# A small gMLP stage beside a stream of K and V loads: x made the stationary operand, one product per group for the row sums

## The chip, the cores and the metric

The kernel runs on one core of a Trainium2 chip. The metric is the device time of one execution in microseconds (us), taken as the median of several executions. All executions told of here were classed as undisturbed (fast); executions of one kernel lie within some 2 us of each other. A ratio below is of one kernel's fast runs to the other's in the same rounds, with a 95% interval; it isn't quite the ratio of the medians quoted beside it. The profile is of one execution; its span is about 2 us shorter than the device time. In its lines PE is TensorE (PEld its weight loads), DVE VectorE, ACT ScalarE, POOL GpSimd and SPq the queue of the sync engine; the clock is the share of TensorE's full clock that it was granted.

## The reference, cut to what matters

One decode step: a layer norm of x (4 rows of 640), then an attention over long caches and a gated MLP side by side, both added to x.

```python
# caches: k, v are (4, 32, 4096, 128) bf16: 268 MB together
q = (xn @ wq).reshape(4, 1, 32, 128).transpose(0, 2, 1, 3)
p = softmax(einsum('bhqd,bhkd->bhqk', q, k_cache) * 128 ** -0.5)
A = einsum('bhqk,bhkd->bhqd', p, v_cache)...reshape(4, 1, 4096) @ wo
z = gelu(xn @ w_in)                      # w_in: 640 x 1728
z1, z2 = z[..., :864], layernorm(z[..., 864:])
B = (z1 * (w_sp * z2 + b_sp)) @ w_out    # w_out: 864 x 640
out = x + A + B
```

The kernel calls the product that w_out multiplies u.

## The kernel before: the parts concerned

The queue of the sync engine loads all but x and two small vectors, in this order: wq, w_in, w_out, then K and V in units of 8 MB (128 rows of 64 KB), and wo. K, V and the weights share five slots of a buffer, so a load can be issued only when the last reader of its slot is done. The gMLP, with 120 small products:

```python
FA = 5                                   # w_out: 5 rows of 640 to each of 128 partitions,
FR = (Fh - FA * P) // 32                 # the rest (7 rows) to each of 32 partitions
...
nc.sync.dma_start(out=w_out, in_=B_w_out[0:nf, :].rearrange("(p c) n -> p c n", p=P))
w_rest_d = B_w_out[nf:Fh, :].rearrange("(i r c) n -> r i c n", r=4, c=FR)
for r in range(4):
    nc.sync.dma_start(out=w_rest[r:32:4], in_=w_rest_d[r])      # 8 rows each
...
zT_ps = misc_ps([P, 2, FC, B], F32)
for part in range(2):
    for fc in range(FC):
        ...
        for c in range(DC):              # w: a strided column block of w_in, stationary
            nc.tensor.matmul(zT_ps[:n, part, fc, :], lhsT=w, rhs=xnT[:, c, 0:B], ...)
nc.scalar.activation(out=zT[:, :, 0:FA, :], in_=zT_ps[:, :, 0:FA, :], func=ACT.Gelu_apprx_tanh)
...                                      # statistics with a ones matrix, Sqrt, u = z1 * t1
etab = const.tile([P, 1], F32)           # loads the Exp table early
nc.scalar.activation(out=etab[:], in_=rs[:, 0:1], func=ACT.Exp)
```

The softmax of a group and what follows it, on whose end the V loads hang:

```python
nc.scalar.activation(out=p_bf[:, :, e, :], in_=S_ps[:, e], func=ACT.Exp, ...)   # per e
nc.vector.transpose(pT[...], p_bf[...])
... # 16 copies pT -> xd, 16 masked copies xd -> Zb (z_fill): VectorE has 11 and 3, ScalarE 5 and 13
for e in range(NE):
    nc.tensor.matmul(cs[:], lhsT=SelPe[:, e]..., rhs=rowsum[:, e:e + 1], ...)
nc.vector.reciprocal(out=rinv[:], in_=cs[:])
```

Of the kernel before, what the change touches and what calls it, by code (L numbers as in the profile page):

```python
# [8 lines left out]
ACT = mybir.ActivationFunctionType  # L9
ALU = mybir.AluOpType  # L10
AX = mybir.AxisListType
F32 = mybir.dt.float32
BF16 = mybir.dt.bfloat16
# [3 lines left out]
def kernel(  # L17
# [19 lines left out]
    nc = tc.nc  # L37
    P = 128
# [5 lines left out]
    HP = 4  # L44
# [9 lines left out]
    G = HG * B  # L54
    F2 = B_w_in.shape[1]
    Fh = F2 // 2
    FA = 5
    FR = (Fh - FA * P) // 32
    assert Fh == FA * P + FR * 32
    FC = FA + FR  # L60
# [20 lines left out]
    def misc_ps(shape, dtype):  # L81
        misc_ctr[0] += 1
        return ps_m.tile(shape, dtype, tag="misc", name=f"misc{misc_ctr[0]}")
# [5 lines left out]
    def at_slot(i, n, off=0):  # L89
        return kv[:, i * SL + off:i * SL + off + n]  # L90
# [12 lines left out]
    nc.scalar.dma_start(out=sb_bf[:, 0:1], in_=B_w_sp)  # L103
    nc.scalar.dma_start(out=sb_bf[:, 1:2], in_=B_b_sp[None, :])

    x_res = const.tile([32, NO2], BF16)
    nc.gpsimd.memset(x_res[:], 0.0)

    wq = at_slot(0, n_q).rearrange("p (c n) -> p c n", c=DC)
# [7 lines left out]
    nc.sync.dma_start(out=w_out, in_=B_w_out[0:nf, :].rearrange("(p c) n -> p c n", p=P))  # L117
    w_rest_t = ktpool.tile([P, NKT], F32, tag="kT", name="w_rest")
    w_rest = w_rest_t[:32].bitcast(BF16)[:, 0:FR * NOUT].rearrange("p (c n) -> p c n", c=FR)
    w_rest_d = B_w_out[nf:Fh, :].rearrange("(i r c) n -> r i c n", r=4, c=FR)  # L120
    for r in range(4):
        nc.sync.dma_start(out=w_rest[r:32:4], in_=w_rest_d[r])
# [88 lines left out]
    for q in range(4):  # L211
        nc.vector.tensor_copy(out=I32[32 * q:32 * q + 32, :], in_=ident_f[32 * q:32 * q + 32, 32 * q:32 * q + 32])

    SelP = const.tile([P, HP * B], F32)
    nc.vector.tensor_reduce(out=SelP[:], in_=I32[:].rearrange("p (pr c) -> p pr c", c=C2), axis=AX.X, op=ALU.add)
    SelN = const.tile([P, HP * B], F32)
    nc.vector.tensor_scalar(out=SelN[:], in0=SelP[:], scalar1=-scale, scalar2=None, op0=ALU.mult)
    SelPe = const.tile([P, NE, HP, NE, B], F32)
    nc.gpsimd.memset(SelPe[:].rearrange("p x h e b -> p (x h e b)"), 0.0)
    for e in range(NE):  # L220
        nc.vector.tensor_copy(out=SelPe[:, e, :, e, :], in_=SelP[:].rearrange("p (h b) -> p h b", b=B))

    SelH = const.tile([P, HG], F32)
    nc.vector.tensor_reduce(out=SelH[:], in_=I32[:].rearrange("p (h c) -> p h c", c=4), axis=AX.X, op=ALU.add)
# [12 lines left out]

    MkH = const.tile([G, HG], F32)
    nc.vector.tensor_reduce(out=MkH[:], in_=ident_f[:G, :G].rearrange("p (h b) -> p h b", b=B), axis=AX.X, op=ALU.add)
    B32f = const.tile([G, B], F32)  # L240
    nc.vector.tensor_reduce(out=B32f[:], in_=ident_f[:G, :G].rearrange("p (h b) -> p b h", b=B), axis=AX.X, op=ALU.add)
    B32 = const.tile([G, B], BF16)
# [30 lines left out]
    nc.vector.tensor_copy(out=qT[:], in_=q4[:, 1, :].rearrange("p (h k r) -> p h k r", h=HG, k=4)[:, :, :, 0:B])  # L273


    zT_ps = misc_ps([P, 2, FC, B], F32)
    for part in range(2):
        for fc in range(FC):
            n = P if fc < FA else 32
            f0 = part * Fh  # L280
            for c in range(DC):
                if fc < FA:
                    w = w_in[:, c, f0:f0 + nf].rearrange("p (f a) -> p a f", a=FA)[:, fc, :]
                else:
                    w = w_in[:, c, f0 + nf:f0 + Fh].rearrange("p (f a) -> p a f", a=FR)[:, fc - FA, :]
                nc.tensor.matmul(zT_ps[:n, part, fc, :], lhsT=w,  # L286
                                 rhs=xnT[:, c, 0:B], start=(c == 0), stop=(c == DC - 1))
    zT = const.tile([P, 2, FC, B], F32)
    nc.gpsimd.memset(zT[:], 0.0)
    uT = const.tile([P, FC, 32], BF16)  # L290
    nc.gpsimd.memset(uT[:], 0.0)
    nc.scalar.activation(out=zT[:, :, 0:FA, :], in_=zT_ps[:, :, 0:FA, :], func=ACT.Gelu_apprx_tanh)
    nc.scalar.activation(out=zT[:32, :, FA:FC, :], in_=zT_ps[:32, :, FA:FC, :], func=ACT.Gelu_apprx_tanh)

    one_bf = const.tile([1, P], BF16)
    nc.gpsimd.memset(one_bf[:], 1.0)
# [1 line left out]
    nc.tensor.matmul(sb_ps[:], lhsT=one_bf[:], rhs=sb_bf[:], start=True, stop=True)  # L298
    sb_f = const.tile([P, 2], F32)
    nc.vector.tensor_copy(out=sb_f[:], in_=sb_ps[:])  # L300
    z1 = zT[:, 0, :, :]
    z2 = zT[:, 1, :, :]
    st_in = const.tile([P, 2, FC, B], F32)
    nc.vector.tensor_copy(out=st_in[:, 0], in_=z2)
    nc.vector.tensor_tensor(out=st_in[:, 1], in0=z2, in1=z2, op=ALU.mult)
    st_ps = misc_ps([P, 2, FC, B], F32)
    nc.tensor.matmul(st_ps[:].rearrange("p s c b -> p (s c b)"), lhsT=ones_f[:],
                     rhs=st_in[:].rearrange("p s c b -> p (s c b)"), start=True, stop=True)
    st = const.tile([P, 2, B], F32)
    nc.vector.tensor_reduce(out=st[:], in_=st_ps[:].rearrange("p s c b -> p s b c"), axis=AX.X, op=ALU.add)  # L310
    mean = const.tile([P, B], F32)
    nc.vector.tensor_scalar(out=mean[:], in0=st[:, 0, :], scalar1=1.0 / Fh, scalar2=None, op0=ALU.mult)
    msq = const.tile([P, B], F32)
    nc.vector.tensor_tensor(out=msq[:], in0=mean[:], in1=mean[:], op=ALU.mult)
    var = const.tile([P, B], F32)
    nc.vector.scalar_tensor_tensor(out=var[:], in0=st[:, 1, :], scalar=1.0 / Fh, in1=msq[:],
                                   op0=ALU.mult, op1=ALU.subtract)
    rs = const.tile([P, B], F32)
    nc.scalar.activation(out=rs[:], in_=var[:], func=ACT.Sqrt, bias=eps_t[:, 0:1], scale=1.0)
    nc.vector.reciprocal(out=rs[:], in_=rs[:])  # L320
    t1 = const.tile([P, FC, B], F32)
    nc.vector.tensor_tensor(out=t1[:], in0=z2, in1=mean[:, None, :].to_broadcast((P, FC, B)),
                            op=ALU.subtract)
    nc.vector.tensor_tensor(out=t1[:], in0=t1[:], in1=rs[:, None, :].to_broadcast((P, FC, B)),
                            op=ALU.mult)
    nc.vector.tensor_scalar(out=t1[:], in0=t1[:], scalar1=sb_f[:, 0:1], scalar2=sb_f[:, 1:2],
                            op0=ALU.mult, op1=ALU.add)
    nc.vector.tensor_tensor(out=uT[:, :, 0:B], in0=z1, in1=t1[:], op=ALU.mult)


    etab = const.tile([P, 1], F32)
    nc.scalar.activation(out=etab[:], in_=rs[:, 0:1], func=ACT.Exp)


    for fc in range(FC):
# [73 lines left out]
    def softmax(g):  # L409
        negmax = softmax_max(g)  # L410
        S_ps = state.pop(("S", g))
        p_bf = ppool.tile([P, TC, NE, M], BF16, tag="p", name="p")
        rowsum = small.tile([P, NE], F32, tag="rowsum")
        for e in range(NE):
            nc.scalar.activation(out=p_bf[:, :, e, :], in_=S_ps[:, e], func=ACT.Exp, bias=negmax[:, e:e + 1], scale=scale,  # L415
                                 accum_out=rowsum[:, e:e + 1])

        pT = ppool.tile([P, TC, HP, B * C2], BF16, tag="p", name="pT")
        nc.vector.transpose(pT[:].rearrange("p t h x -> p (t h x)"), p_bf[:].rearrange("p t e m -> p (t e m)"))  # L419

        xd = small.tile([P, B * C2, 4, TC], BF16, tag="xd", name="xd", bufs=1)
        state[("xd", g)] = xd
        for hp in range(HP):
            for q in range(4):
                op = nc.vector.tensor_copy if q < 2 or (hp < 3 and q == 2) else nc.scalar.copy
                op(out=xd[32 * hp:32 * hp + 32, :, q, :], in_=pT[32 * q:32 * q + 32, :, hp, :].rearrange("p t x -> p x t"))  # L426
        z_fill(g, 0)
        z_fill(g, 1)
        cs = misc_ps([G, 1], F32)
        for e in range(NE):  # L430
            nc.tensor.matmul(cs[:], lhsT=SelPe[:, e].rearrange("p h e b -> p (h e b)"), rhs=rowsum[:, e:e + 1],  # L431
                             start=(e == 0), stop=(e == NE - 1))
        rinv = small.tile([G, 1], F32, tag="rinv")
        nc.vector.reciprocal(out=rinv[:], in_=cs[:])
        state[("rinv", g)] = rinv

    def emit_V(v):
# [49 lines left out]
    for i, item in enumerate(seq):  # L487
        if i + 1 < len(seq):
            key, u = seq[i + 1]
            if u == NU - 2 and key == "v":  # L490
                x_rows = x_flat.rearrange("b (h n) -> (b h) n", h=NH)
                for r0, r1 in ((0, 3), (3, 2 * B)):
                    nc.sync.dma_start(out=x_res[4 * r0:4 * r1:4, :], in_=x_rows[r0:r1])
            load_unit(seq[i + 1])
            if key == "k" and u == 2 * B - 1:
                load_wo(u // B - 1)
        else:
            load_wo(NG - 3)
            load_wo(NG - 2)
            load_wo(NG - 1, (0, 4, 6, 7, 8))  # L500
# [15 lines left out]
                softmax(g)  # L516
        else:
            emit_V(u)
            if u == NU - 2:
                for hf in range(NH):  # L520
                    nc.tensor.matmul(proj[32 * hf:32 * hf + B, 0:NO2], lhsT=ident_bf[:32, 4 * hf:32:8], rhs=x_res[:],
                                     start=False, stop=False)
    emit_proj(NG - 3)
    emit_sel(NG - 1)
    emit_proj(NG - 2, range(0, 4))
# [1 line left out]
    emit_proj(NG - 2, range(4, HG))  # L527

    o_1 = ppool.tile([64, NO2], F32, tag="p", name="o_1")
    nc.vector.tensor_copy(out=o_1[:], in_=proj[0:64, 0:NO2])  # L530
    nc.vector.tensor_tensor(out=o_1[:], in0=proj[64:128, 0:NO2], in1=o_1[:], op=ALU.add)
    last = ps_l.tile([64, NO2], F32)
    oT = state[("oT", NG - 1)]
# [39 lines left out]
```

## Time and profile before

665.66 us, median of 3 runs (665.23 to 665.97).

| | before |
|---|---|
| span of the profile | 663.9 us |
| moved by the load queue | 282.25 MB, 425 GB/s |
| DMA engines busy | 90% or more in 39 of 40 slices |
| DVE, PE, ACT busy | 54%, 45%, 12% |
| gMLP: first product to last | 21.07 to 34.7 us |
| third K load, which overwrites the gMLP's weights, issued | 52.06 us |

How to read it: no compute engine is the bound, though DVE at 54% looks the most likely; the transfer engines are. One stretch of the timeline it reasons about but doesn't show is the first softmax. Columns: start, duration (us), engine, line, operation, output and inputs, count.

```profile
119.56 1.23 DVE L379 TENSOR_REDUCE m<-S 128x2 f32<-128x1024 f32 x1 [1.22 <-PE S L372]
...
123.08 0.69 ACT L415 ACTIVATE p<-S,negmax 128x512 bf16<-128x512 f32 x1 [90.19 <-DVE negmax L393]
...
131.56 6.47 PE L443 MATMUL O<-kv,Zb 128*32 128x512 bf16 x64 [6.70 <-ACT Zb L407]
135.20 0.33 SPq L158 DMA_DIRECT2D kv<-in_A_v_cache_dram  x1
```

From the maximum of the scores (119.56) to the V load that may be issued once half of the first V unit is used (135.20): 15.64 us.

### The profile page before, as it was taken

The numbers are of one execution on the slowest core, as the hardware profiler recorded it, in microseconds if no ns is written. First come the engines' busy times: TensorE is split into PE (matmuls) and PEld (weight loads), VectorE is DVE, ScalarE is ACT, GpSimd is POOL, SyncE is SP. The second block draws the span as 40 slices with busy tenths as digits, with TensorE's granted clock in tenths as the row PEclk, the third lists the DMA queues.
The fourth block names the chain that finished last, engine by engine and source line by source line (L and its number), as shares of the span: only waits on it lengthen the run. The fifth ranks groups of instructions, "written<-read, shape, count | busy, mean of one in ns | idle before, by whom it ended". The sixth has DMA issues, their size and how long they took to land.

```text
span 663.9 us, 5636 instructions
## 1 busy us (share of the span) xinstructions
PE 298.9 (45%) x2394; PEld 112.8 (17%) x2394; DVE 360.7 (54%) x331; ACT 77.8 (12%) x162; POOL 10.2 (2%) x35
## 2 busy tenths in 40 slices
PE   0624765266072556225446175542506254633245
PEld 0401211122021122101112022110202112211012
DVE  5248999656190849509164286745628084950002
ACT  0300000430100000530200000070100000062200
POOL 3000000000000000000000000000000000000000
PEclk9998778768576587677757676766958768777767
DMA  9999999999999999999999999999999999999995
GB/s 372 461 434 416 423 451 434 430 435 435 415 442 435 430 414 440 440 430 431 438 438 431 426 422 436 440 438 435 426 430 427 434 433 420 452 431 428 425 414 229
DMA packets 6901, 282.61 MB, mean 426 GB/s; under 512 B 808, under 2 KB 1084, under 8 KB 1468
## 3 DMA queue, kind: packets, MB, share of 16 engines
q1 hardware_dynamic: 6856, 282.25, 98.6%
q8 instruction: 18, 0.29, 0.2%
q14 instruction: 7, 0.06, 0.0%
q10 hardware_dynamic: 20, 0.01, 0.0%
HBM read 282.25 MB, written 0.01 MB: 425 GB/s over the span
## 4 chain that ended last, share of the span: by engine, by line
DMA 71%; issue 12%; DVE 12%; PE 3%; ACT 1%; DVEq 0%; SPq 0%; ACTq 0%
DMA kv<-in_A_k_cache_dram 61%; DVE kT L361 11%; DMA kv<-in_A_v_cache_dram 5%; DMA kv<-in_A_wo_dram 3%; DMA kv<-in_A_wq_dram 2%; PE O L443 2%; PE q L262 1%; PE S L372 0%; ACT xd L426 0%; ACT Zb L407 0%; PE last L538 0%; ACT p L415 0%; DVE pT L419 0%; DVE kv L271 0%; DVE m L379 0%
## 5 line engine op out<-in xcount | busy, mean ns | idle before, releaser
L361 DVE STREAM_TRANSPOSE kT<-kv 128x2048 f32<-128x2048 f32 x128 | 282.8, 2275 | 127.4 <-DMA kv<-in_A_k_cache_dram 125.7
L372 PE MATMUL S<-kT,QZ 128*32 128x512 bf16 x1024 | 190.2, 505 | 232.5 <-DVE kT L361 232.5
L372 PEld LDWEIGHTS <-QZ 128*32 128x32 bf16 x1024 | 61.0, 112 | 356.5 <-issue 337.6
L443 PE MATMUL O<-kv,Zb 128*32 128x512 bf16 x1024 | 75.9, 462 | 59.8 <-DMA kv<-in_A_v_cache_dram 32.8
L450 DVE TENSOR_SCALAR R<-O,Mk 128x128 f32<-128x128 f32 x16 | 5.6, 350 | 126.9 <-PE O L443 126.9
L407 ACT ACTIVATE Zb<-xd,MkE 32x256 bf16<-32x256 bf16 x116 | 52.9, 498 | 109.2 <-PE O L443 107.7
L415 ACT ACTIVATE p<-S,negmax 128x512 bf16<-128x512 f32 x8 | 5.4, 682 | 402.0 <-DVE negmax L393 402.0
L443 PEld LDWEIGHTS <-Zb 128*32 128x32 bf16 x1024 | 33.3, 114 | 101.7 <-issue 60.9
L460 PE MATMUL misc<-R,SelR 128*32 128x128 f32 x32 | 6.4, 281 | 26.0 <-DVE R L452 26.0
L452 DVE SCALAR_TENSOR_TENSOR R<-O,Mk,R 128x128 f32<-128x128 f32 x48 | 16.8, 351 | 1.7
L426 DVE COPY xd<-pT 32x256 bf16<-32x256 bf16 x44 | 16.1, 365 | 0.7
L426 ACT COPY xd<-pT 32x256 bf16<-32x256 bf16 x20 | 12.2, 612 | 5.6 <-DVE pT L419 5.2
L347 POOL COPY QZ<-qT 32x32 bf16<-32x32 bf16 x16 | 5.1, 317 | 418.6 <-PE S L372 400.2
L419 DVE STREAM_TRANSPOSE pT<-p 128x1024 bf16<-128x1024 bf16 x4 | 5.0, 1245 | 6.6 <-ACT p L415 6.6
L460 PEld LDWEIGHTS misc<-R,SelR 128*32 128x32 f32 x32 | 2.2, 107 | 33.5 <-DVE R L452 24.8
L379 DVE TENSOR_REDUCE m<-S 128x2 f32<-128x1024 f32 x4 | 4.9, 1224 | 5.5 <-PE S L372 5.5
L286 PE MATMUL misc<-xnT,kv 128*32 128x4 bf16 (+1 forms) x120 | 6.2, 188 | 0.7 <-DMA kv<-in_B_w_in_dram 0.7
L286 PEld LDWEIGHTS <-kv 128*32 128x32 bf16 (+1 forms) x120 | 6.1, 142 | 1.6 <-DMA kv<-in_B_w_in_dram 1.6
L431 PE MATMUL misc<-rowsum,SelPe 128*32 128x1 f32 x16 | 2.0, 197 | 9.3 <-ACT p L415 9.3
L262 PE MATMUL q<-kv,xnT 128*32 128x512 bf16 x40 | 4.5, 631 | 3.9 <-DMA kv<-in_A_wq_dram 3.9
L463 DVE SCALAR_TENSOR_TENSOR om<-misc,rinv,MkH 32x1024 bf16<-32x1024 f32 x4 | 5.1, 1271 | 2.0 <-PE misc L460 2.0
L384 PE MATMUL misc<-dg,ones_f 128*128 128x256 f32 x8 | 2.7, 416 | 7.5 <-DVE dg L381 7.5
(96 smaller groups left out, 63.6 us busy)
## 6 DMA issues: line engine op xcount, KB each, us to landing
kv<-in_A_k_cache_dram SPq DMA_DIRECT2D x8, 4096.0 KB
kv<-in_A_v_cache_dram SPq DMA_DIRECT2D x1, 6144.0 KB
kv<-in_A_wq_dram SPq DMA_DIRECT2D x1, 5120.0 KB
kv<-in_A_wo_dram SPq DMA_DIRECT2D x3, 1280.0 KB
kv<-in_B_w_in_dram SPq DMA_DIRECT2D x1, 2160.0 KB, 19.8
kv<-in_A_v_cache_dram SPq DMA_DIRECT2D x1, 2048.0 KB
kv<-in_B_w_out_dram SPq DMA_DIRECT2D x1, 800.0 KB
kv<-in_A_wo_dram SPq DMA_DIRECT2D x1, 640.0 KB, 22.5
```

The lines of the kernel that those rows point to most:

```text
L262: nc.tensor.matmul(q4_ps[32 * j:32 * j + 32, hf * 512:hf * 512 + 512], lhsT=xnT[:, c, :], rhs=wq[:, c, n0:n0 + 512], start=(c == 0), stop= ...
L286: nc.tensor.matmul(zT_ps[:n, part, fc, :], lhsT=w, rhs=xnT[:, c, 0:B], start=(c == 0), stop=(c == DC - 1))
L347: nc.gpsimd.tensor_copy(out=QZ[r0:r0 + 32, :, :, :, 8 + 8 * hp], in_=qT[32 * g:32 * g + 32, NE * hp:NE * hp + NE].rearrange("p e a b -> p ...
L361: nc.vector.transpose(kT[:].rearrange("p (t r) -> p t r", r=32), kw)
L372: nc.tensor.matmul(S_ps[32 * q:32 * q + 32, e], lhsT=QZ[:, b, 2 * kh + w, e, w0:w0 + 32], rhs=kb[:, i, :, e, :, w], start=(b == 0 and k < ...
L407: nc.scalar.activation(out=dst, in_=src, func=ACT.Copy, scale=mk)
L415: nc.scalar.activation(out=p_bf[:, :, e, :], in_=S_ps[:, e], func=ACT.Exp, bias=negmax[:, e:e + 1], scale=scale, accum_out=rowsum[:, e:e + 1])
L426: op(out=xd[32 * hp:32 * hp + 32, :, q, :], in_=pT[32 * q:32 * q + 32, :, hp, :].rearrange("p t x -> p x t"))
L443: nc.tensor.matmul(O_ps[32 * q:32 * q + 32, :, :], lhsT=Zb[b % 2][:, w].rearrange("p h c -> p (h c)"), rhs=vv[:, w * 4 * Dh:(w + 1) * 4 * ...
L450: nc.vector.tensor_scalar(out=R, in0=O_ps[:, 0, :], scalar1=Mk4[:, 0:1], scalar2=None, op0=ALU.mult)
L452: nc.vector.scalar_tensor_tensor(out=R, in0=O_ps[:, c, :], scalar=Mk4[:, c:c + 1], in1=R, op0=ALU.mult, op1=ALU.add)
L460: nc.tensor.matmul(oh[:], lhsT=SelR[:, b].rearrange("p h b -> p (h b)"), rhs=state["R"][:, b, :], start=(b == 0), stop=(b == B - 1))
```

## The change

The intent: fewer and larger products in the gMLP. x is the stationary operand (32 columns, 4 of them used) and w_in streams past it in four column tiles; u comes out with the batch on partitions and is turned by a 32x32 vector transpose. For its layout w_out is cut 6 + 3 instead of 5 + 7. The row sums of a group take one product in place of two, the residual x is added at the evacuation in place of by two products, and the Exp warm-up no longer waits for the gMLP.

```diff
-    FA = 5
+    FA = 6
...
-    zT_ps = misc_ps([P, 2, FC, B], F32)
-    for part in range(2):
-        for fc in range(FC):
-            ...  # 120 matmuls, w stationary
+    for c in range(DC):
+        for q in range(4):
+            nc.tensor.matmul(z_ps[32 * q:32 * q + 32], lhsT=xnT[:, c, :], rhs=w_za[:, c, q], ...)
+        nc.tensor.matmul(zr_ps[:], lhsT=xnT[:, c, :], rhs=w_zr[:, c], ...)
+    z_f = at_slot(2, 2 * 3 * NB, z_at)...     # z, u live in slot 2, behind w_out
...
-    st_ps ... ones_f, PSUM reduce
+    nc.vector.tensor_reduce(out=st_in[:, 0:1], in_=z2, ...)      # and of z2 * z2
+    nc.tensor.matmul(st_ps[:], lhsT=I4..., rhs=st_in[:], start=True, stop=True)
...
+    nc.vector.transpose(z_b[:, 1, :], z_b[:, 0, :])
-    nc.scalar.activation(out=etab[:], in_=rs[:, 0:1], func=ACT.Exp)
+    nc.scalar.activation(out=etab[:], in_=eps_t[:], func=ACT.Exp)
...
-        for e in range(NE):
-            nc.tensor.matmul(cs[:], lhsT=SelPe[:, e]..., rhs=rowsum[:, e:e + 1], ...)
-        nc.vector.reciprocal(out=rinv[:], in_=cs[:])
+        nc.tensor.matmul(cs[:], lhsT=SelP2..., rhs=rowsum[:], start=True, stop=True)
+        nc.vector.tensor_tensor(out=cm[:], in0=cs[:], in1=MkG[:], op=ALU.mult)
+        nc.vector.tensor_reduce(out=rinv[:], in_=cm[:], axis=AX.X, op=ALU.add)
+        nc.vector.reciprocal(out=rinv[:], in_=rinv[:])
...
-            if u == NU - 2:   # x into proj by two matmuls
-                ...
-    nc.vector.tensor_copy(out=o_1[:], in_=proj[0:64, 0:NO2])
+    nc.vector.tensor_tensor(out=o_1[:], in0=proj[0:64, 0:NO2], in1=x_res[:], op=ALU.add)
```

More of the change, by code (lines that the diff above doesn't have):

```diff
@@ L104 @@
     nc.scalar.dma_start(out=sb_bf[:, 1:2], in_=B_b_sp[None, :])
-    x_res = const.tile([32, NO2], BF16)
+    x_res = const.tile([64, NO2], BF16)
     nc.gpsimd.memset(x_res[:], 0.0)
@@ L119 @@
     w_rest = w_rest_t[:32].bitcast(BF16)[:, 0:FR * NOUT].rearrange("p (c n) -> p c n", c=FR)
+    NB = 32 * FC
+    z_at = n_in + FA * NOUT
     w_rest_d = B_w_out[nf:Fh, :].rearrange("(i r c) n -> r i c n", r=4, c=FR)
@@ L212 @@
         nc.vector.tensor_copy(out=I32[32 * q:32 * q + 32, :], in_=ident_f[32 * q:32 * q + 32, 32 * q:32 * q + 32])
+    I4 = const.tile([P, 4, 32], F32)
+    nc.gpsimd.tensor_copy(out=I4[:], in_=I32[:, None, :].to_broadcast((P, 4, 32)))
     SelP = const.tile([P, HP * B], F32)
@@ L217 @@
     nc.vector.tensor_scalar(out=SelN[:], in0=SelP[:], scalar1=-scale, scalar2=None, op0=ALU.mult)
-    SelPe = const.tile([P, NE, HP, NE, B], F32)
-    nc.gpsimd.memset(SelPe[:].rearrange("p x h e b -> p (x h e b)"), 0.0)
-    for e in range(NE):
-        nc.vector.tensor_copy(out=SelPe[:, e, :, e, :], in_=SelP[:].rearrange("p (h b) -> p h b", b=B))
+    SelP2 = const.tile([P, HP, NE, B], F32)
+    nc.vector.tensor_copy(out=SelP2[:], in_=SelP[:].rearrange("p (h b) -> p h b", b=B)[:, :, None, :].to_broadcast((P, HP, NE, B)))
     SelH = const.tile([P, HG], F32)
@@ L239 @@
     nc.vector.tensor_reduce(out=MkH[:], in_=ident_f[:G, :G].rearrange("p (h b) -> p h b", b=B), axis=AX.X, op=ALU.add)
+    MkG = const.tile([G, NE], F32)
+    nc.vector.tensor_reduce(out=MkG[:], in_=MkH[:].rearrange("p (h e) -> p e h", e=NE), axis=AX.X, op=ALU.add)
     B32f = const.tile([G, B], F32)
@@ L273 @@
     nc.vector.tensor_copy(out=qT[:], in_=q4[:, 1, :].rearrange("p (h k r) -> p h k r", h=HG, k=4)[:, :, :, 0:B])
-    zT_ps = misc_ps([P, 2, FC, B], F32)
-    for part in range(2):
-        for fc in range(FC):
-            n = P if fc < FA else 32
-            f0 = part * Fh
-            for c in range(DC):
-                if fc < FA:
-                    w = w_in[:, c, f0:f0 + nf].rearrange("p (f a) -> p a f", a=FA)[:, fc, :]
-                else:
-                    w = w_in[:, c, f0 + nf:f0 + Fh].rearrange("p (f a) -> p a f", a=FR)[:, fc - FA, :]
-                nc.tensor.matmul(zT_ps[:n, part, fc, :], lhsT=w,
-                                 rhs=xnT[:, c, 0:B], start=(c == 0), stop=(c == DC - 1))
-    zT = const.tile([P, 2, FC, B], F32)
-    nc.gpsimd.memset(zT[:], 0.0)
-    uT = const.tile([P, FC, 32], BF16)
-    nc.gpsimd.memset(uT[:], 0.0)
-    nc.scalar.activation(out=zT[:, :, 0:FA, :], in_=zT_ps[:, :, 0:FA, :], func=ACT.Gelu_apprx_tanh)
-    nc.scalar.activation(out=zT[:32, :, FA:FC, :], in_=zT_ps[:32, :, FA:FC, :], func=ACT.Gelu_apprx_tanh)
+    w_z = w_in.rearrange("p c (a f) -> p c a f", a=2)
+    z_ps = misc_ps([P, 2, FA, 32], F32)
+    zr_ps = misc_ps([32, 2, FR, 32], F32)
+    w_za = w_z[:, :, :, 0:nf].rearrange("p c a (q j i) -> p c q a i j", q=4, j=32)
+    w_zr = w_z[:, :, :, nf:Fh].rearrange("p c a (j i) -> p c a i j", j=32)
+    for c in range(DC):
+        for q in range(4):
+            nc.tensor.matmul(z_ps[32 * q:32 * q + 32], lhsT=xnT[:, c, :], rhs=w_za[:, c, q], start=(c == 0), stop=(c == DC - 1))
+        nc.tensor.matmul(zr_ps[:], lhsT=xnT[:, c, :], rhs=w_zr[:, c], start=(c == 0), stop=(c == DC - 1))
+    z_f = at_slot(2, 2 * 3 * NB, z_at).bitcast(F32).rearrange("p (a n) -> p a n", a=3)
+    z_b = at_slot(2, 2 * NB, z_at + 6 * NB).rearrange("p (a n) -> p a n", a=2)
+    zT = z_f[:, 0:2, :].rearrange("p a (i j) -> p a i j", j=32)
+    nc.gpsimd.memset(z_f[:, 0:2, :], 0.0)
+    nc.scalar.activation(out=zT[:, :, 0:FA, :], in_=z_ps[:], func=ACT.Gelu_apprx_tanh)
+    nc.scalar.activation(out=zT[:32, :, FA:FC, :], in_=zr_ps[:], func=ACT.Gelu_apprx_tanh)
     one_bf = const.tile([1, P], BF16)
@@ L300 @@
     nc.vector.tensor_copy(out=sb_f[:], in_=sb_ps[:])
-    z1 = zT[:, 0, :, :]
-    z2 = zT[:, 1, :, :]
-    st_in = const.tile([P, 2, FC, B], F32)
-    nc.vector.tensor_copy(out=st_in[:, 0], in_=z2)
-    nc.vector.tensor_tensor(out=st_in[:, 1], in0=z2, in1=z2, op=ALU.mult)
-    st_ps = misc_ps([P, 2, FC, B], F32)
-    nc.tensor.matmul(st_ps[:].rearrange("p s c b -> p (s c b)"), lhsT=ones_f[:],
-                     rhs=st_in[:].rearrange("p s c b -> p (s c b)"), start=True, stop=True)
-    st = const.tile([P, 2, B], F32)
@@ L310 @@
-    nc.vector.tensor_reduce(out=st[:], in_=st_ps[:].rearrange("p s c b -> p s b c"), axis=AX.X, op=ALU.add)
-    mean = const.tile([P, B], F32)
-    nc.vector.tensor_scalar(out=mean[:], in0=st[:, 0, :], scalar1=1.0 / Fh, scalar2=None, op0=ALU.mult)
-    msq = const.tile([P, B], F32)
+    z1, z2, t1 = z_f[:, 0, :], z_f[:, 1, :], z_f[:, 2, :]
+    st_in = const.tile([P, 2], F32)
+    nc.vector.tensor_reduce(out=st_in[:, 0:1], in_=z2, axis=AX.X, op=ALU.add)
+    nc.vector.tensor_tensor(out=t1, in0=z2, in1=z2, op=ALU.mult)
@@ L314 @@
+    nc.vector.tensor_reduce(out=st_in[:, 1:2], in_=t1, axis=AX.X, op=ALU.add)
+    st_ps = misc_ps([P, 2], F32)
+    nc.tensor.matmul(st_ps[:], lhsT=I4[:].rearrange("p q k -> p (q k)"), rhs=st_in[:], start=True, stop=True)
+    mean = const.tile([P, 1], F32)
+    nc.vector.tensor_scalar(out=mean[:], in0=st_ps[:, 0:1], scalar1=1.0 / Fh, scalar2=None, op0=ALU.mult)
+    msq = const.tile([P, 1], F32)
     nc.vector.tensor_tensor(out=msq[:], in0=mean[:], in1=mean[:], op=ALU.mult)
-    var = const.tile([P, B], F32)
@@ L316 @@
-    nc.vector.scalar_tensor_tensor(out=var[:], in0=st[:, 1, :], scalar=1.0 / Fh, in1=msq[:],
+    var = const.tile([P, 1], F32)
+    nc.vector.scalar_tensor_tensor(out=var[:], in0=st_ps[:, 1:2], scalar=1.0 / Fh, in1=msq[:],
                                    op0=ALU.mult, op1=ALU.subtract)
-    rs = const.tile([P, B], F32)
+    rs = const.tile([P, 1], F32)
     nc.scalar.activation(out=rs[:], in_=var[:], func=ACT.Sqrt, bias=eps_t[:, 0:1], scale=1.0)
     nc.vector.reciprocal(out=rs[:], in_=rs[:])
-    t1 = const.tile([P, FC, B], F32)
@@ L322 @@
-    nc.vector.tensor_tensor(out=t1[:], in0=z2, in1=mean[:, None, :].to_broadcast((P, FC, B)),
-                            op=ALU.subtract)
-    nc.vector.tensor_tensor(out=t1[:], in0=t1[:], in1=rs[:, None, :].to_broadcast((P, FC, B)),
-                            op=ALU.mult)
-    nc.vector.tensor_scalar(out=t1[:], in0=t1[:], scalar1=sb_f[:, 0:1], scalar2=sb_f[:, 1:2],
-                            op0=ALU.mult, op1=ALU.add)
-    nc.vector.tensor_tensor(out=uT[:, :, 0:B], in0=z1, in1=t1[:], op=ALU.mult)
+    nc.vector.tensor_scalar(out=t1, in0=z2, scalar1=mean[:, 0:1], scalar2=rs[:, 0:1], op0=ALU.subtract, op1=ALU.mult)
@@ L331 @@
+    nc.vector.tensor_scalar(out=t1, in0=t1, scalar1=sb_f[:, 0:1], scalar2=sb_f[:, 1:2], op0=ALU.mult, op1=ALU.add)
+    nc.vector.tensor_tensor(out=z_b[:, 0, :], in0=z1, in1=t1, op=ALU.mult)
+    nc.vector.transpose(z_b[:, 1, :], z_b[:, 0, :])
+    uT = z_b[:, 1, :].rearrange("p (i r) -> p i r", r=32)
     etab = const.tile([P, 1], F32)
-    nc.scalar.activation(out=etab[:], in_=rs[:, 0:1], func=ACT.Exp)
+    nc.scalar.activation(out=etab[:], in_=eps_t[:], func=ACT.Exp)
     for fc in range(FC):
@@ L428, in softmax @@
         z_fill(g, 1)
-        cs = misc_ps([G, 1], F32)
-        for e in range(NE):
-            nc.tensor.matmul(cs[:], lhsT=SelPe[:, e].rearrange("p h e b -> p (h e b)"), rhs=rowsum[:, e:e + 1],
-                             start=(e == 0), stop=(e == NE - 1))
+        cs = misc_ps([G, NE], F32)
+        nc.tensor.matmul(cs[:], lhsT=SelP2[:].rearrange("p h e b -> p (h e b)"), rhs=rowsum[:], start=True, stop=True)
+        cm = small.tile([G, NE], F32, tag="cm")
+        nc.vector.tensor_tensor(out=cm[:], in0=cs[:], in1=MkG[:], op=ALU.mult)
         rinv = small.tile([G, 1], F32, tag="rinv")
-        nc.vector.reciprocal(out=rinv[:], in_=cs[:])
+        nc.vector.tensor_reduce(out=rinv[:], in_=cm[:], axis=AX.X, op=ALU.add)
+        nc.vector.reciprocal(out=rinv[:], in_=rinv[:])
         state[("rinv", g)] = rinv
@@ L490 @@
             if u == NU - 2 and key == "v":
-                x_rows = x_flat.rearrange("b (h n) -> (b h) n", h=NH)
-                for r0, r1 in ((0, 3), (3, 2 * B)):
-                    nc.sync.dma_start(out=x_res[4 * r0:4 * r1:4, :], in_=x_rows[r0:r1])
+                for hf in range(NH):
+                    nc.sync.dma_start(out=x_res[32 * hf:32 * hf + B, :], in_=x_flat[:, hf * NO2:(hf + 1) * NO2])
             load_unit(seq[i + 1])
@@ L518 @@
             emit_V(u)
-            if u == NU - 2:
-                for hf in range(NH):
-                    nc.tensor.matmul(proj[32 * hf:32 * hf + B, 0:NO2], lhsT=ident_bf[:32, 4 * hf:32:8], rhs=x_res[:],
-                                     start=False, stop=False)
     emit_proj(NG - 3)
```

## The prediction

> **What bounds the kernel now.** I read the page first (slices, queues, chain), then the chain of waits in order of time, then what the load queue waited for, then the timeline around the changed lines. The page settles most of it:
>
> ```profile
> span 663.9 us, 5636 instructions
> ...
> DMA  9999999999999999999999999999999999999995
> GB/s 372 461 434 416 423 451 434 430 435 435 415 442 435 430 414 440 440 430 431 438 438 431 426 422 436 440 438 435 426 430 427 434 433 420 452 431 428 425 414 229
> ...
> q1 hardware_dynamic: 6856, 282.25, 98.6%
> ```
>
> Every slice but the last has the 16 DMA engines 90% busy or more, and the one load queue accounts for 98.6% of their time. 282.25 MB in 663.9 us is 425 GB/s. The 1.4% left over (9.3 us) is about 2 us before the first packet and the tail, in which engines finish one after another and the last matmuls and the store follow. So there is no hole in the middle for a faster compute stage to close; a change pays only if it removes bytes, moves the first packet, shortens the tail or evens out the engines.
>
> The chain, in order of time, shows the only place where the gMLP's inputs come near it, and the tail:
>
> ```profile
> 0.73 15.19 DMA kv<-in_A_wq_dram
> ...
> 15.96 4.48 PE q L262 x30
> ...
> 23.37 40.30 DMA kv<-in_A_k_cache_dram
> ...
> 635.91 22.53 DMA kv<-in_A_wo_dram
> ...
> 658.49 2.33 PE last L538 x16
> ...
> 660.90 0.48 DVE o_bf L542
> ```
>
> The chain goes through q, which the change leaves alone, into the second K load at 23.37 us. The gMLP is not on it. Who could feel the gMLP? The third K load, which overwrites its weights. The load queue's own timeline has it at 52.06:
>
> ```profile
> 52.06 0.33 SPq L158 DMA_DIRECT2D kv<-in_A_k_cache_dram  x1
> ```
>
> The queue's waits name the K transposes (kT, L361) for it, not the gMLP. The gMLP's last products, in the timeline:
>
> ```profile
> 21.07 6.21 PE L286 MATMUL misc<-xnT,kv 128*128 128x4 bf16 x120 [0.65 <-DMA kv<-in_B_w_in_dram]
> ...
> 33.45 1.23 PE L340 MATMUL proj<-w_rest,uT 32*4 32x320 bf16 x14
> ```
>
> They end at 34.7 us. So the gMLP has 52.06 - 34.7 = 17.4 us of slack before the change.
>
> **What the Trainium skill says.** "DMA: Bandwidth & Descriptors", section "Where 436 GB/s comes from", puts the ceiling of the 16 engines at 435.2 GB/s; the trace agrees (426 GB/s mean, slices of 430 to 440). The same page, "Why a DMA increments its semaphore by 16 and not by 1", says that a load from the sync queue is spread over the largest k up to 16 that divides its row count, on the lowest-numbered k engines. So an 8-row load uses only 8. The trace's packet records agree: the four 8-row w_rest loads are 32 packets of 8,960 B, 338 ns each, and where I could follow lanes they stand four in a row, 340 ns apart. "ScalarE: Activation LUTs", "What ACT_TABLE_LOAD costs", gives about 1283 ns for a table load; the three in this stage take 1283 ns each. "TensorE: Matmul & The Clock Gate", "Wait - 56ns, not 53.3ns?", gives N / 1.2 GHz from start to start on the throttled clock; for 320 columns that is 267 ns, and the last 16 matmuls (8 pairs, each pair side by side) start 267 ns apart in the trace, at granted clock 0.50.
>
> **The change part by part.**
>
> *The z product.* Removed: 120 matmuls of 4 moving columns, 6.2 us. Added: 20 matmuls of 384 columns over four column tiles and 5 of 192. The q product is the same form: 40 of 512 columns in 4.46 us, 446 ns per four. Hence 5 x 446 x 384/512 = 1.7 us, plus 5 x 167 ns = 0.8 us: 2.5 us, so -3.7 us.
>
> *gelu, statistics, u.* Columns per operation go from 48 to 288, because only 4 of each 32 hold data. Rows for the size: TENSOR_TENSOR and TENSOR_REDUCE of 128x256 f32 take 0.42 us, so about 0.46 us at 288 (the small ones took 0.2); a 1024-column bf16 transpose takes 1.25 us, so 0.35 us at 288. Two gelus grow by about 0.5 us in all (the 512-column exp takes 0.68). Sums: one TENSOR_TENSOR and two reduces, 1.4 us, for 0.3; the matrix product for statistics is smaller (-0.3), the PSUM reduce is gone (-0.26); u costs +0.55 and its transpose +0.35. Together about +1.9 us.
>
> *The output product.* 18 matmuls for 24, over 2.15 us: -0.5 us.
>
> So the gMLP gets about 3.7 - 1.9 + 0.5 = 2.3 us shorter, ending near 32.4 us. It has 17.4 us of slack already: worth 0. Its buffers now lie in slot 2 behind w_out, the slot that is free only after the same stage, so they add no new wait.
>
> *Exp table.* The instruction order shows the warm-up exp moved ahead of gelu and sqrt; those throw its table out, so the first softmax loads it again. One extra load early (about 10.5 us, ACT is free until 21.19), and one on the path of the first softmax, +1.28 us.
>
> *Row sums.* One product for two per group, but a multiply by a mask and a small reduce are added on DVE between the transpose and the copies: about 0.2 + 0.2 us, +0.4 us per softmax at most, -0.1 on PE.
>
> These two delay V product 0 by up to 1.7 us, and so the load at 135.20 that waits for it. The load before it was issued at 109.60 and lands at 141.3 (the chain: 31.70 us), so 6.1 us are in hand; 4.4 remain. In the last group the load at 599.75 is issued 11.5 us before the previous V lands (its products start at 611.26). Worth 0.
>
> *Start.* GpSimd now builds a broadcast identity from what DVE makes at 9.5 us, and the SelR memset queues behind it; DVE's SelR copies (10.1 us) wait perhaps 0.5 us, and with them xnT (12.13). The q product waits for wq until 15.96: 3.3 us left. Worth 0.
>
> *The residual.* Two matmuls (0.30 us) go from a stretch where PE then idles 12 us; the evacuation becomes an add of the same size (0.48 against 0.49 us), done at 659.3, needed at 660.9. Worth 0.
>
> *Layout of w_out.* The one term I can find on the path. Bytes stay. w_out rows grow from 6,400 to 7,680 B (8 per engine), w_rest packets shrink from 8,960 to 3,840 B (4 on each of 8 engines). Packets of 6,400, 8,960 and 17,280 B take 244, 338 and 644 ns, a line of 36.8 ns per 1,000 B and 9 ns; so 7,680 B take 291 and 3,840 B 150. Eight engines change by 8 x 47 - 4 x 188 = -0.38 us, the other eight by +0.38 us. All carry equal K and V shares, in queues never empty, so an engine's lead or lag lasts to the end, and the end waits for the slowest. Following packets by their gaps I get lanes ending up to 5.7 us apart, the last two among the eight that carry w_rest, the best of the others 1.1 us ahead of the last. Then the end moves by about -0.3 to -0.4 us. That reconstruction has doubtful links, and another run may have another slowest engine.
>
> **Sum:** 665.66 + 0 + (-0.3) = 665.4 us.
>
> **Rivals.**
> 1. *A new wait in the first softmax.* The extra table load and DVE steps could make a load late. For it: the load at 135.20 hangs directly on that product. Against it: 6.1 us in hand against 1.7. If the delay were three times what I expect (5.1 us) it would still be hidden; beyond 6.1 each us would cost one.
> 2. *The gMLP frees the queue earlier and the span drops by its 2.3 us.* For it: PE does less in a stage with 6 us of matmuls. Against it: the third K load waits for transposes until 52.06, and the engines are full. It would give 663.4; I give it little.
> 3. *The other eight engines become slowest,* or w_rest sits on fast ones: +0.4 us, 666.0.
> 4. *The tail's clock.* If different PE work left the clock full in the last matmuls, 2.33 would fall towards 1.2 us: 664.3. Against it: the product before them is unchanged, and what precedes the last 20 us is the same load-paced pattern.
>
> **Range and chances.** The three runs of before lie within 0.74 us; a median of three moves by perhaps 0.3, the engine term by 0.4 either way. 664.6 to 666.3 should hold it 8 times in 10. Two per cent is 13.3 us, more than the whole tail or the whole of the gMLP's matmuls: faster 0.01, same 0.98, slower 0.01.
>
> **What would show it.** Right: DMA 90% or more in 39 slices, the same 282.25 MB; the gMLP's last product near 32 us and the third K load still near 52; a table load of 1.28 us ahead of the first p, the V load near 137 instead of 135.2 and no dip of GB/s after it; last matmuls still at clock 0.50 for 2.3 us. Wrong: a third K load waiting for the gMLP's reads, a slice under 9 around 140 us, or a wo landing more than 1 us from 658.45.

## The result, and the profile after

665.1 us, median of 4 runs (664.79 to 665.46), against 665.82 us for the kernel before in the same comparison (665.23 to 666.35, 4 runs). The ratio is 0.999, interval 0.9972 to 1.0007: the same, by the rule of 2%, and a difference of 0.7 us that its own interval doesn't tell from zero.

The page of the changed kernel, in the lines that answer to those of before:

```profile
span 663.0 us, 5426 instructions
...
DMA  9999999999999999999999999999999999999996
GB/s 370 463 440 428 407 438 441 439 428 436 428 435 432 431 415 446 431 435 436 427 439 436 427 416 446 437 439 428 415 440 439 436 439 406 453 420 433 429 416 253
...
q1 hardware_dynamic: 6856, 282.25, 98.8%
```

The same bytes, the same full engines: 210 instructions are gone, and in the DMA row only the last digit differs, 6 for 5. The gMLP in the timeline of the changed kernel:

```profile
21.17 0.68 PE L291 MATMUL misc<-kv,xnT 128*32 128x384 bf16 x4 [1.11 <-DMA kv<-in_B_w_in_dram]
...
25.83 0.49 ACT L297 ACTIVATE kv<-misc 128x384 f32<-128x384 f32 x1
...
31.23 0.48 DVE L327 STREAM_TRANSPOSE kv<-kv 128x288 bf16<-128x288 bf16 x1
...
32.69 0.69 PE L340 MATMUL proj<-w_rest,kv 32*4 32x320 bf16 x6
```

It ends at 33.38 us in place of 34.7, and the third K load, whose line follows, doesn't move with it: 52.51 against 52.06. That load still ends a wait for K transposes. (In this run the chain of waits goes through the transposes straight to it.)

```profile
52.51 0.33 SPq L161 DMA_DIRECT2D kv<-in_A_k_cache_dram  x1
```

The first softmax has the expected new line, a table load of 1.28 us that waits for the same event as p did:

```profile
118.86 1.22 DVE L379 TENSOR_REDUCE m<-S 128x2 f32<-128x1024 f32 x1 [1.22 <-PE S L372]
...
122.31 1.28 ACT L415 ACT_TABLE_LOAD   x1 [92.73 <-DVE negmax L393]
123.60 0.69 ACT L415 ACTIVATE p<-S,negmax 128x512 bf16<-128x512 f32 x1
...
135.71 0.33 SPq L161 DMA_DIRECT2D kv<-in_A_v_cache_dram  x1
```

From the maximum to the V load it is now 135.71 - 118.86 = 16.85 us, 1.21 more than before. The extra steps for the row sums cost nothing here: the multiply (0.11 us) fits before the copies and the small reduce falls after them.

The tail, from the chain of waits:

```profile
635.17 22.47 DMA kv<-in_A_wo_dram
...
657.67 2.30 PE last L534 x16
...
660.06 0.48 DVE o_bf L538
```

The last products start 0.82 us earlier than before and still take 2.30 us. What moved is the landing of wo ahead of them.

### The profile page after: what moved, and what is told of

Its sections match the earlier page's. It is cut to its first block, busy times and chain, and to the rows that moved or that the text cites. A ratio compares the mean times of both kernels' runs of the same rounds, so it can differ in the third digit from the quotient of the medians.

```text
span 663.0 us, 5426 instructions
## 1 busy us (share of the span) xinstructions
PE 289.5 (44%) x2283; PEld 106.4 (16%) x2283; DVE 362.0 (55%) x339; ACT 79.5 (12%) x163; POOL 10.7 (2%) x34
## 4 chain that ended last, share of the span: by engine, by line
DMA 74%; DVE 11%; issue 11%; PE 2%; ACT 1%; SPq 0%; DVEq 0%; ACTq 0%
DMA kv<-in_A_k_cache_dram 64%; DVE kT L361 11%; DMA kv<-in_A_v_cache_dram 4%; DMA kv<-in_A_wo_dram 3%; DMA kv<-in_A_wq_dram 2%; PE O L444 2%; ACT xd L426 0%; ACT Zb L407 0%; PE last L534 0%; PE S L372 0%; ACT p L415 0%; DVE pT L419 0%; DVE m L379 0%; PE misc L384 0%; SPq L125 0%
## 5 line engine op out<-in xcount | busy, mean ns | idle before, releaser
L372 PE MATMUL S<-kT,QZ 128*32 128x512 bf16 x1024 | 188.3, 500 | 239.0 <-DVE kT L361 239.0
```

Source lines behind the costliest of these rows:

```text
L372: nc.tensor.matmul(S_ps[32 * q:32 * q + 32, e], lhsT=QZ[:, b, 2 * kh + w, e, w0:w0 + 32], rhs=kb[:, i, :, e, :, w], start=(b == 0 and k < ...
```

## The experiments

The theory: time is the bytes, and how evenly the 16 engines carry them; every compute part of the change is hidden, the Exp reload too, but by a margin; the layout of w_out alone is on the path, by 0.3 to 0.4 us. The rivals: compute parts that reach the end, a margin that isn't there, and noise.

Twelve kernels ran. Each gave the reference's result except the two that are wrong on purpose.

### e1 and e2: the layout alone, the compute alone

```diff
 # e1: the kernel before          # e2: the changed kernel
-    FA = 5                       -    FA = 6
+    FA = 6                       +    FA = 5
```

> The kernel before with only the cut of w_out changed (6 rows of 640 to a partition instead of 5; the old z product, old statistics, old row sums). Theory (the layout of w_out is the only part of the change on the path): 0.3 to 0.4 us below before, as the whole change. Rival 1 (the compute parts make the difference): equal to before within 0.1 us. Rival 2 (the difference of 0.7 us between before and after is noise between runs): equal to before, with an interval as wide as the difference.

> The changed kernel with the old cut of w_out (5 rows to a partition). Theory (layout): equal to before within 0.1 us, that is about 0.4 us above the changed kernel. Rival 1 (compute): as the changed kernel, 0.7 us below before. Rival 2 (noise): equal to before. The last V load of the first softmax's product should be issued near 135.7 us, as in the changed kernel, since the Exp reload stays.

Measured, 5 runs each beside 9 of before (median 665.17): e1 665.09 us, ratio 0.9997 (0.9984 to 1.0009); e2 666.03 us, ratio 1.0006 (0.9994 to 1.0019). The order is that of the theory, the layout on the fast side and the compute alone on the slow side, but both intervals hold 1 and are wider than the 0.4 us in question. The pair gives no support to the compute rival and doesn't settle layout against noise. The trace of e2 also has its V load after the first softmax late, at 136.55; what that costs, e7 makes clear.

### e5 and e6: the stage taken away, then bytes taken away

```diff
 # e5: the changed kernel without z, gelu, statistics, u (result wrong on purpose)
-    ... 25 matmuls, 2 gelus, all DVE work of the stage
+    nc.gpsimd.memset(z_b[:, 1, :], 0.0)      # u = 0; loads and output products stay
 # e6: e5, and
-    nc.sync.dma_start(out=w_in, in_=B_w_in.rearrange("(p c) f -> p c f", c=DC))
```

> The changed kernel without the gMLP's z product, gelu, statistics and u (25 matmuls, 2 gelus, all of the DVE work of the stage; u is set to zero, so the result is wrong on purpose); all loads stay. Theory (the stage is hidden, 12 us of it are worth nothing): as the changed kernel, 665.1 us within 0.4. Rival (the stage's PE, ACT and DVE time reaches the end in part): 1 us or more below.

> As e5, and w_in isn't loaded either (2.21 MB; wrong result on purpose). Theory (bytes are the time: 8 packets of 17,280 B and 644 ns per engine): 5.2 us below e5, near 660. Rival (the first K load waits for wq to land and leaves a hole that the w_in load fills today): only 2 to 4 us below.

Measured: e5 665.16 us (4 runs; before 665.22, 7 runs; ratio 1.0000, 0.9985 to 1.0015). e6 660.93 us, ratio 0.9938 (0.9923 to 0.9953). In the trace of e5 the gMLP's last product starts at 24.42 us, 8.3 us before that of the changed kernel:

```profile
23.50 0.99 PE L305 MATMUL proj<-kv 128*32 128x320 bf16 x12 [3.28 <-DMA kv<-in_B_w_out_dram]
24.42 0.69 PE L305 MATMUL proj<-w_rest,kv 32*4 32x320 bf16 x6
```

So a whole stage of work is worth nothing, within the 1.0 us to either side that the interval leaves, and its 2.21 MB are worth 4.2 us. That is the shape of a transfer bound, and it bounds what any rewrite of this stage that leaves its loads alone can bring. Without the stage's gelu and Sqrt e5 has no Exp reload either: its V load goes out at 134.81, 15.58 us after the maximum, as in the kernel before. The reload is thus covered by the same zero. The 5.2 us expected of e6 were not reached in full. Part of the rest is the small hole that the rival named; the windows of 2 us around the first K load in e6 show it (columns: window, length, busy time of PE, PEld, DVE, ACT, POOL, clock, DMA share, GB/s; a packet counts where it starts, so neighbours must be read together):

```profile
16.00:18.00 2.00, 2.00 (x20) 0.83 (x23) 0.00 (x0) 0.00 (x0) 0.00 (x0) 1.00 1.80 693
18.00:20.00 2.00, 2.00 (x36) 0.92 (x28) 0.24 (x1) 0.00 (x0) 0.00 (x0) 1.00 0.24 98
```

Laid out by the packets' own times, the engines idle 0.30 us on average between 17 and 19 us in e6 and not at all in e5. The 4.9 us that this leaves of the 5.2 lie within the interval (3.1 to 5.1 us).

### e7 and e8: the first softmax delayed

```diff
+        if g == 0:
+            for _ in range(5):               # e8: 20
+                nc.scalar.activation(out=scr[:], in_=S_ps[:, 0], func=ACT.Exp, bias=negmax[:, 0:1], scale=scale)
         p_bf = ppool.tile([P, TC, NE, M], BF16, tag="p", name="p")
```

> The changed kernel with 5 more exps of 128x512 (about 0.6 us each, written to a scratch tile) between the maximum and p in the first softmax: its V product, and the V load that waits for it, move by 3.0 us, from 135.7 to 138.7. Theory (about 5 us in hand before the load before it has landed, at 140.7): no change, within 0.4 us. Rival (the queue has less in hand than the landing suggests): up to 3 us more.

> As e7 with 20 exps, 12 us: the V load would be issued at 147.7, 7 us after the load before it has landed. Theory (the hand is 5 us, the rest is a hole in the DMA that nothing fills later): 7 to 9 us more than the changed kernel, and a stretch of idle DMA near 141 to 149. Rival (later slack absorbs it): under 2 us.

Measured: e7 666.00 us, ratio 1.0013 (0.9998 to 1.0028). e8 676.86 us, ratio 1.0177 (1.0160 to 1.0194). The exps took 0.72 us each, not 0.6, so the V load moved by 3.2 us in e7 (to 138.93) and by 14.3 in e8 (to 149.99), where 3.0 and 12 were meant. The first line below is a row of the timeline of e8, the others are its windows:

```profile
123.61 14.37 ACT L415 ACTIVATE scr<-S,negmax 128x512 bf16<-128x512 f32 x20
```

```profile
130.00:135.00 5.00, 0.00 (x0) 0.00 (x0) 0.00 (x0) 4.77 (x8) 0.00 (x0) 0.50 1.00 433
135.00:140.00 5.00, 0.27 (x2) 0.18 (x2) 0.65 (x1) 4.18 (x9) 0.00 (x0) 0.50 0.52 223
140.00:145.00 5.00, 0.00 (x0) 0.00 (x0) 4.78 (x14) 4.21 (x8) 0.00 (x0) 0.50 0.00 0
145.00:150.00 5.00, 3.66 (x36) 1.40 (x40) 0.99 (x5) 4.87 (x11) 0.00 (x0) 0.50 0.02 5
```

The DMA share falls to 0 and stays there until the V load is issued. A hole in the stream is paid in full: 14.3 us later, 11.7 us longer (676.86 - 665.22 = 11.64; 1.0177 gives 11.8). What was in hand in the changed kernel is the difference, about 2.5 us (1.4 to 3.6 by the interval of e8), and not the 5 that the landing of the load before suggests. e7 agrees, but its interval holds 1: 3.2 later, 0.8 longer by the medians, so 2.4 in hand. Its windows have the dip that before and after lack:

```profile
135.00:140.00 5.00, 4.37 (x56) 1.83 (x60) 0.34 (x3) 4.19 (x10) 0.00 (x0) 0.66 0.76 305
140.00:145.00 5.00, 1.54 (x20) 0.65 (x14) 4.23 (x6) 3.61 (x8) 0.00 (x0) 1.00 0.89 354
```

By packet times the engines of e7 idle 1.4 us on average between 138 and 141 us; in the profiled runs of before and after no microsecond of this stretch idles more than 1/16. In the other kernels with the reload (e3 apart) the V load went out between 135.57 (e9) and 136.60 (e4), and the engines idle between nothing (e4) and 0.4 us (e2, issued at 136.55). In the changed kernel the first engines are thus near running dry, though the time of the kernel grows only with a later load.

The theory had too large a margin. e8 shows it: 14.3 us late with 5 in hand would have cost 9.3, and 11.7 were paid (of the excess over the 7 to 9 expected, 2.3 us come from the longer exps). e7's no change isn't refuted, its interval reaching from -0.1 to +1.9 us. The packets of e8 show where the count fails. Its 16 engines finish the K load between 138.0 and 140.0 us, where the changed kernel sees that load landed at 140.7, and the first packets of the V load start 1.0 us after its issue.

### e9: the gMLP delayed, which failed

```diff
     nc.scalar.activation(out=zT[:, :, 0:FA, :], in_=z_ps[:], func=ACT.Gelu_apprx_tanh)
+    scr = const.tile([P, 2, FA, 32], BF16)
+    for _ in range(75):
+        nc.scalar.activation(out=scr[:], in_=z_ps[:], func=ACT.Gelu_apprx_tanh)
     nc.scalar.activation(out=zT[:32, :, FA:FC, :], in_=zr_ps[:], func=ACT.Gelu_apprx_tanh)
```

> The changed kernel with 75 more gelus of 128x384 (about 0.41 us each, 31 us in all, to a scratch tile) inside the gMLP's chain, whose last product then ends near 64 us instead of 33.4. Theory A (the first S products stand behind the gMLP's products in PE's order, so the K transposes, and with them the third K load at 52, slip by 64 - 45.6 = 19 us; the queue runs dry at 63): 8 to 10 us more. Theory B (as the prediction counted it, slack up to the third K load alone: the load is issued at 64): 2 to 4 us more. Rival (hidden wholly): no change.

Measured: 664.70 us, ratio 0.9997 (0.9981 to 1.0013). That is no answer to the question: the build is free to reorder, and put 69 of the 75 gelus behind the square root, where nothing waits for them. The timeline of e9:

```profile
30.64 0.29 ACT L325 ACTIVATE rs<-var,eps_t 128x1 f32<-128x1 f32 x1
...
32.25 36.03 ACT L300 ACTIVATE scr<-misc 128x384 bf16<-128x384 f32 x69
33.13 0.99 PE L343 MATMUL proj<-kv 128*32 128x320 bf16 x12 [4.15 <-DVE kv L330]
34.05 0.69 PE L343 MATMUL proj<-w_rest,kv 32*4 32x320 bf16 x6
```

The last product slipped by 1.4 us only. What e9 shows instead is that 36 us of ScalarE work from 32 to 68 us, beside the loads, cost nothing that the runs can tell (1 us). How late the gMLP may be before the third K load suffers stays untested; theories A and B of the expectation are both open.

### e11 and e12: an unequal and an equal share for the engines

```diff
 # in load_unit, after the load of a K unit
+        if key == "k" and u in (4, 5, 6, 8, 9, 10, 12, 13, 14):
+            for r in range(4):                                                   # e11
+                nc.sync.dma_start(out=scr[r:32:4], in_=src[8 * r:8 * r + 8, 0:2048])
+            nc.sync.dma_start(out=scr[:], in_=src[:, 0:512])                     # e12 instead
```

> The changed kernel with nine extra dummy loads of 128 KB behind K loads, each as four loads of 8 rows of 4 KB (partitions 0, 4, 8, ... as w_rest), so that eight engines get 36 packets of about 157 ns more and eight get none. Theory (an engine's lag is kept to the end and the end waits for the slowest): 5.6 us more than the changed kernel, less what those eight are ahead, so 4 to 5.7. Rival (shares even out): half, 2.8 us. Third view (the extra issues disturb the order of the queue): more than 6 us.

> The control of e11: the same nine times 128 KB, each as one load of 128 rows of 1 KB over all 16 engines: 72 packets of about 46 ns more on each. Theory and rival alike: 3.3 us more than the changed kernel (2.8 us if only bytes count). If e11 costs about 2 us more than this, the unequal share is what costs; if e11 costs the same, it isn't.

Measured beside the same 9 runs of before (median 665.31): e11 670.77 us, ratio 1.0083 (1.0069 to 1.0097), +5.5 us; e12 668.15 us, ratio 1.0044 (1.0031 to 1.0056), +2.9 us. The same bytes cost almost twice as much when eight engines carry them alone. The eight got 36 packets of 159 ns, 5.7 us; the 5.5 us paid are nearly that, so shares don't even out by the end, though the extra packets run between 138 and 538 us and the kernel goes on for 130 us after the last. The windows of the tail show what happens, e11 first:

```profile
655.00:660.00 5.00, 2.73 (x48) 1.13 (x40) 2.67 (x5) 0.00 (x0) 0.00 (x0) 1.00 0.75 307
660.00:665.00 5.00, 3.44 (x40) 2.00 (x40) 1.17 (x3) 0.00 (x0) 0.00 (x0) 0.68 0.22 82
```

```profile
655.00:660.00 5.00, 2.16 (x34) 1.39 (x38) 2.43 (x5) 0.00 (x0) 0.00 (x0) 0.90 0.88 359
660.00:665.00 5.00, 3.16 (x32) 1.30 (x20) 1.46 (x3) 0.00 (x0) 0.00 (x0) 0.50 0.17 60
```

In e11 the share is 0.75 between 655 and 660 us where e12 (below) still has 0.88: the engines that carried nothing extra are presumably the ones that are done (a packet record doesn't name its engine), and e11 then drags on with the others. No microsecond between 145 and 645 us idles in either kernel. This is the mechanism that the layout term of the prediction rests on, at some fifteen times its size.

### e4: w_rest over 16 engines

```diff
-    for r in range(4):
-        nc.sync.dma_start(out=w_rest[r:32:4], in_=w_rest_d[r])
+    nc.sync.dma_start(out=w_rest, in_=B_w_out[nf:Fh, :].rearrange("(p c) n -> p c n", c=FR))
```

> The changed kernel with w_rest as one load of 32 rows over 16 engines instead of four loads of 8 rows over 8: eight engines lose two packets of 150 ns (-0.3 us), eight gain two (+0.3 us). Theory (layout, slowest engine among the eight): up to 0.3 us faster than the changed kernel, less where an engine of the other eight becomes the last. Rival (engine balance doesn't matter): equal within 0.1 us.

Measured: 665.32 us, ratio to before 1.0001 (0.9988 to 1.0013). No gain is seen, and none of 0.3 us could be.

### e3: one K load cut into 120 and 8 rows

```diff
-            nc.sync.dma_start(out=unit(item, t0, t1), in_=src[:, t0 * Dh:t1 * Dh])
+            cut = (0, 120, P) if item == ("k", B) else (0, P)
+            for p0, p1 in zip(cut[:-1], cut[1:]):
+                nc.sync.dma_start(out=unit(item, t0, t1)[p0:p1], in_=src[p0:p1, t0 * Dh:t1 * Dh])
```

> The changed kernel with one K load (8 MB) cut into a load of 120 rows and one of 8 rows. If row counts decide the engines as the packets suggest, eight engines carry one 64 KB row more (2.42 us, the duration of such a packet), seven the same, one eight rows less. Theory (an engine's lag lasts to the end, the end waits for the slowest engine, and the slowest is one of the eight that carry w_rest): the span grows by 1.5 to 2.5 us over the changed kernel. Rival (the engines' shares even out over the 550 us that follow, or the end does not hang on the slowest engine): within 0.5 us.

Measured: 698.63 us, ratio 1.0501 (1.0487 to 1.0516): 33 us for one cut in one of 32 units, and neither view had it. The page of e3 shows three slices at half the rate or less, with the engines busy nearly all the time (one sixteenth idles from 120 to 138 us, as if 15 of 16 worked):

```profile
DMA  9999999999999999999999999999999999999995
GB/s 377 466 430 422 421 443 399 196 208 154 433 420 433 430 441 414 443 434 426 445 422 434 437 430 418 442 426 438 441 438 426 419 433 428 454 426 424 438 406 228
```

Packets of 64 KB, 2.42 us elsewhere, took 5.10 us (median) from 119 to 150 us, those of the V load behind it included. The Trainium skill offers a reason: "DMA: Bandwidth & Descriptors", section "Why a DMA increments its semaphore by 16 and not by 1", gives 15 engines to 120 rows, and "SBUF — State Buffer", section "Door 1: The DMA port swizzle", ties partitions to ports in such a way that eight rows in a run for each engine would put two engines on one port at a time. The factor of 2.1 agrees, but this reason doesn't explain all: by it the engine with rows 88 to 95 would share with none in this load, yet no 64 KB packet that started from 120 to 150 us took under 4.79 us, and those that started from 156 to 164 took up to 10.8. No run here tests it; the cause stays open. The cut was also two changes in one, a load of 120 rows and one of 8. As a test of the engine shares e3 was no use, and e11 took its place.

### e10: PE kept busy ahead of the last products

```diff
+    keep_warm(6, ...last V chunk)     # 128-column identity times 512 columns, result unused
     emit_proj(NG - 3)
     ...
     emit_oT(NG - 1)
+    keep_warm(3, om_w)
     emit_proj(NG - 2, range(4, HG))
+    keep_warm(4, wo_t[NG - 2][:, HG - 1, 0:512])
```

> The changed kernel with 13 idle matmuls of 512 columns in PE's gaps of the last 7 us, to keep the granted clock full until the last 16 matmuls (2.3 us at half clock). Theory (those 16 are on the path and run 133 ns apart at full clock): the last matmuls take 1.2 to 1.6 us, 0.5 to 1.0 us less than the changed kernel, so faster than both kernels. Rival (the last wo packets land late enough to hold the last pair anyway, or the clock drops all the same): within 0.2 us.

Measured: 665.22 us, ratio 0.9997 (0.9984 to 1.0009). The clock did stay full; the windows of 2 us, the changed kernel first, then e10 (the column before the last two is the clock):

```profile
658.00:660.00 2.00, 1.97 (x16) 0.86 (x11) 0.00 (x0) 0.00 (x0) 0.00 (x0) 0.50 0.07 27
```

```profile
658.00:660.00 2.00, 1.55 (x16) 0.59 (x12) 0.26 (x2) 0.00 (x0) 0.00 (x0) 1.00 0.05 19
```

The last 16 products took 1.81 us, not 1.2: pairs 136 ns apart at first, then three waits, each before the first pair that reads a further piece of wo. Half a microsecond of PE time was freed, the late packets took part of it back, and the time of the kernel doesn't show the rest above its noise. No version here that gives the right result beats both kernels by more than can be told.

## Why the prediction was right

The prediction said 665.4 us, 664.6 to 666.3, the same; the median is 665.1. By its steps:

- **The bound.** Right, and now shown from both sides: a stage without its work is worth 0 within 1.0 us (e5), 2.21 MB less are worth 4.2 us (e6), and a hole of the queue is paid in full (e8). (Its "slices of 430 to 440" are 414 to 461 between the first and the last; the mean of 425 is right.)
- **The gMLP's own time.** It ends 1.3 us sooner, not 2.3. The z product is off: 21.17 to 24.56, 3.4 us against 2.5. Its five rounds stand 0.65 us apart, where the prediction's 0.33 for four products of 384 columns and 0.17 for the one of 192 make 0.50; the excess is in the fours (0.50 us from their start to that of the 192-column product, then 0.15 to the next round), and the last product's 0.31 us in full comes on top. Why the fours take longer than q's isn't shown. From the start of gelu to u it takes 5.88 us (25.83 to 31.71) against 3.82 before (28.66 to 32.48), 2.1 us more where 1.9 were counted. None of it reaches the end, as e5 shows.
- **The Exp reload.** Right in place and size: 1.28 us of load, 1.21 us more to the V load (1.16 to 1.23 in e2, e4, e9, e10 and e11, too; 1.75 in e12). The row sums were put at up to 0.4 us and cost nothing.
- **The slack at that V load.** Right that it hides the delay, wrong in size. "6.1 us are in hand ... 4.4 remain" took the landing of the load before as the moment when the queue runs dry; e7 and e8 put what remains at about 2.5 us. Rival 1, which the prediction let go up to a delay of 6.1 us, would have begun to cost at about half of that. The conclusion held because the delay, 1.2 us, was smaller than either count.
- **The tail.** Right: clock 0.50, 2.30 us, the residual's add unseen.
- **The layout of w_out, -0.3 to -0.4 us.** The packet times it was built from came out as worked out (291 ns for 7,680 B; 149 for 3,840 B, put at 150), and e11 against e12 shows that a share carried by eight engines stays with them to the end. That this is the cause of the 0.7 us between the medians isn't shown: e1, e2 and e4 have intervals of about 0.8 us to either side and can't resolve 0.4. It stays open. That the median lies 0.3 us from the figure predicted is no support for the term: without it the sum is 665.7, as near to the runs within their noise.
- **The chances.** The 0.98 on "same" rested on 13.3 us being more than all that could move. e5 supports it.

## What to carry to other kernels

When one queue keeps all transfer engines full from end to end, look for a stage's cost in what it does to the issue of the next load (here, the tail apart, nothing else was found); take the stage out once (wrong result, same loads) and you know, within the noise, what a rewrite of its work can bring. Count the margin of a load from the moment the engines run dry and not from the landing of the load before: here 2.5 us were in hand where the landing said 5. And look at how the rows of a load fall on the engines: one load of 120 + 8 rows in place of 128 cost 33 us, far more than the work that was tuned beside it.

## What the Trainium skill lacked or had wrong

- "DMA: Bandwidth & Descriptors" tells how many engines a load gets, and "SBUF — State Buffer" which port a partition is on; neither says that a load of 120 rows in 64 KB pieces, followed by one of 8, halves the rate: 5.10 us a packet against 2.42, those of the load behind them included, 33 us in all (e3).
- "DMA: Bandwidth & Descriptors" gives a fixed cost per load and its causes, but not how to count the slack of a queue: a load issued at 138.93, in a kernel where about 5 us seemed left at 135.7, left the engines idle 1.4 us on average (e7).
- The same page doesn't say that unequal shares persist: 1.18 MB on eight engines cost 5.5 us, on sixteen 2.9 us (e11, e12).
- "ScalarE: Activation LUTs", "What ACT_TABLE_LOAD costs", puts a switch at 2.66 us with its drain. In the first softmax here it moved p by its 1.28 us alone, and the V load by 1.21.
- The same section lets back-to-back activations overlap by 93 ns, from which 0.61 us is the estimate for a 512-column one with a bias pointer and 0.41 us for one of 384 columns without. Writing one scratch tile again and again they took 0.72 us each (e8, 14.37 us for 20) and 0.52 us (e9, 36.03 us for 69), so no overlap is seen.
